# Attention followed by two expert layers on one core: one block of experts beside the attention instead of two, and the third block by seven products

## The chip, the core and the metric

The kernel runs on one core of a Trainium2 chip. The time is the device time of one execution, in microseconds (us); smaller is better. PE is TensorE (matrix products), PEld its weight loads, DVE is VectorE, ACT is ScalarE, POOL is GpSimd, SP is SyncE, which issues the transfers.

## What is computed

An attention with a window of 32 and 32 global tokens per batch, then two layers of the form gate, value, output ("experts") on all 2176 tokens of 512 features, with 1536 hidden features each. Cut to what matters:

```python
x = attention(q_l, k_l, v_l, q_g, k_g, v_g)      # 2176 x 512
xn = x / sqrt(mean(x * x) + 1e-6) * rms_g
g = xn @ w1_gate                                   # 512 x 1536
x = (g * sigmoid(g) * (xn @ w1_val)) @ w1_out      # 1536 x 512
out = (sigmoid(x @ w2_gate) * (x @ w2_val)) @ w2_out
```

All inputs are float64 words in memory, which the kernel turns into float32 and then into pairs of float16 (a high and a low part), so that each product takes three float16 matmuls.

## The kernel before, in words

**Tiling.** The tokens are 17 tiles of 128 (tile 16 holds the global rows). Each expert layer's 1536 hidden features are cut into six blocks of 256; there are 12 blocks, 0 to 11, of which 0 to 5 are the first layer. A block has three weight matrices: gate, value and output.

**Two ways of multiplying a block.** Blocks below `GS` (line 90, 3 before) go in the plain way: the tokens in six chunks of three tiles (the last of two), and for each chunk 48 matmuls for gate and value (`gv_mm`, line 311) and 24 for the output (`out1`, line 496). The output of a chunk comes one chunk late: `flush`, line 1161, is called after the first half (j = 0) of the next chunk. Blocks from `GS` on go through `quad_gv` (line 385): the tokens in three parts of 6, 6 and 5 tiles, each cut in two halves, and gate and value each from seven products of half size in place of eight, that is 84 matmuls of 384 columns (320 for the third part) at line 364, and 48 of the same width for the output. The seven products need sums and differences of the tokens, made once per layer (`x_combos`, line 603, and `combos`, line 579: for each part and each of two halves of the features one group of seven jobs, 42 jobs in all; lines 613, 587, 593 and 596 on POOL, DVE and ACT), and of the weights (`sums`, `sums2` in `w_block`, lines 249 to 255).

**After a half chunk** (`gv_post`, line 322) ACT applies the gate, DVE multiplies, ACT makes the high part and POOL the low part `hlo` (line 343). The output matmuls of `out1` need `hlo` as their second operand already. While attention steps are left, the gate is a Tanh with two products on DVE (lines 337 to 340); after that it is a Silu with one (lines 333, 334).

**Order.** Every engine gets its instructions in an order that the program writes out, and runs them in that order. The attention is a list of 318 steps (about 19 per tile). The first 93 (`n0`, line 1132) run before any expert work. Then the chunks of the list `work` (the list `first`, line 1087, then the chunks of block 2) are emitted one by one, and the function `tick` (line 1106), called 12 times per chunk (four times in each half, four times in `out1`), deals out the rest: at every `pace[2]`-th tick one job of `x_combos`, at every `pace[1]`-th tick one step of the weights' preparation (`w_step`, line 290, from the list that `w_block` fills: ten steps for a plain block, sixteen for one with seven products), and so many attention steps that each chunk's tokens are ready when it comes (`due`, line 1091, from the order of `first`). Counting this through by hand gives, for the order before, 61, 23, 22, 23, 23, 23, 22, 20 and 8 attention steps in the chunks 0 to 8, and none after. `x_combos` enters its jobs when the attention is out of steps, at the start of chunk 9.

**Weights.** DVE shifts and joins the words of the weights (lines 151, 154, 157), ACT makes the high part (line 187), DVE the low part (line 190). `w_need` runs what is missing at once when a block is about to start; `j_need`, line 542, does the same for the token sums before the first block with seven products.

Of the kernel before, what the change touches and what calls it, by code (L numbers as in the profile page):

```python
# [19 lines left out]
def tile_attention_moe_moe(  # L20
# [59 lines left out]
    chunks_b = [(i, o * 128, n * 128) for i, o, n in ((0, 0, 3), (0, 3, 3), (1, 0, 3), (1, 3, 3), (2, 0, 3), (2, 3, 2))]  # L80
# [6 lines left out]
    w_src = [(w1_gate, w1_val, w1_out), (w2_gate, w2_val, w2_out)]  # L87
    wide = w1_gate.dtype == mybir.dt.int64

    GS = 3  # L90

    GP = 6
    raw_t = []
# [80 lines left out]
    def w_half(n, j):  # L174
        w_ahead(2 * n + (j + 3 if wide else 2))
        if wide:
            if len(w_words.get(n, [])) <= j:
                w_scale(n)
            w_bits(n, j, 0)
            w_bits(n, j, 1)  # L180
            w_scale(n + j)
            w_ahead(2 * n + j + 4)
            if j == 1:
                w_words.pop(n)
# [12 lines left out]
    def w_block(g):  # L197
        w_done[g] = [False, False]

        def mark(i):  # L200
            w_done[g][i] = True
# [3 lines left out]
        def small(f):  # L205

            def f2():
                f()
                w_step()
            return f2  # L210

        def late():
            while w_late:
                w_lo(*w_late.pop())

        def conv(w):
            n = 3 * g + w
            if g < GS:
                return [lambda: (late(), w_half(n, 0)), lambda: w_half(n, 1)]
            return [lambda: (late(), w_conv1(n)), lambda: w_conv2(n)]  # L220
# [9 lines left out]

        if g < GS:
            def alloc():
                w_t[g] = [hp.tile([128, 2, 2, 2, DM], F16, tag="wgv", name="wgv"), None]
# [45 lines left out]
        def alloc_o():  # L279
            w_t[g][1] = (hp if g < GS else pb[1]).tile([128, 2, 2, DM], F16, tag="wo", name="wo", bufs=2 if g < GS else 3)  # L280

        jobs += conv(2) + [small(alloc_o), plain(2, lambda: [w_t[g][1][:, :, a] for a in range(2)])]
        if g < GS:
            jobs.insert(wgv_done + 1, small(lambda: mark(0)))
# [799 lines left out]
            pos[0] += 1  # L1084


    first = [(0, 0, 3), (0, 3, 3), (1, 0, 3), (1, 3, 3), (0, 6, 3), (1, 6, 3), (0, 9, 3), (1, 9, 3), (0, 12, 3), (0, 15, 2), (1, 12, 3), (1, 15, 2)]

    MARGIN = 2400
    due = []  # L1090
# [1 line left out]
    work = []  # L1092
# [4 lines left out]
        xi, o = x_place(T)  # L1097
        work.append((g, (xi, o * 128, n * 128), T + n - 1))
    due = due[1:]
    work += [(g, ch, None) for g in range(2, GS) for ch in chunks_b]  # L1100
    clock = [0, 0.0]


    pace = [0, 2, 3]

    def tick(n):
        pace[0] += 1
# [19 lines left out]
    with tc.manual_schedule():  # L1127
        load_k(0)
        load_q(0)
        load_k(1)  # L1130
        setup()
        n0 = done[2] + 4
        W0 = 16
        acts = {
            "kg": lambda: gsrc.update(k=load_g(k_g)),
            "gB": lambda: nc.sync.dma_start(out=gB, in_=rms_g.partition_broadcast(128)),
            "q1": lambda: load_q(1),
            "qg": lambda: gsrc.update(q=load_g(q_g)),
            "v0": lambda: load_v(0),
            "v1": lambda: load_v(1),  # L1140
            "v2": lambda: load_v(2),
            "vg0": lambda: load_vg(0),
            "vw0": lambda: start_vw(0),
            "vw1": lambda: start_vw(1),
            "w0": w_load,
            "w1": w_load,
            "w2": w_load,
        }
        plan = [[0, 'qg'], [3, 'v0'], [8, 'w0'], [0, 'kg'], [0, 'q1'], [4, 'vg0'], [8, 'vw0'], [9, 'w2'], [10, 'gB'], [8, 'w1'], [0, 'v1'], [10, 'v2'], [15, 'vw1']]
        w_block(0)  # L1150
        plan += [(W0 + (n0 - W0) * i // 11, w_step) for i in range(11)]
        plan += [(i, lambda n=n: warm(n)) for i, n in enumerate([13, 2, 2, 2, 2, 10])]
        for i, a in sorted(plan, key=lambda x: x[0]):
            run_to(min(i, n0))
            (acts[a] if isinstance(a, str) else a)()
        run_to(n0)
        clock[1] = float(n0)

        w_block(1)

        def flush():

            while pend:
                g, key = pend.pop(0)
                if g == group[g][-1]:
                    outs(g, key)
                if 0 < g < GS and key in (2, chunks_b[-1], last.get(g)):
                    w_block(g + 2)
                    pace[1] = [2, 4, 3, 3, 4, 4, 4, 2, 4, 2, 2, 2][g]
                if g == NBLK - 1:  # L1170
                    if isinstance(key, int):
                        y_combos(key)
                    elif key[1] > 0:
                        y_combos(key[0])

        last = {g: [w[1] for w in work if w[0] == g][-1] for g in range(2)}
        for wi, (g, ch, ci) in enumerate(work):
            if ci is not None:
                run_to(done[ci])
                clock[1] = max(clock[1], float(pos[0]))  # L1180
            if pos[0] == len(steps) and not pb:
                st_at.close()
                pb[1] = st_p1.enter_context(tc.tile_pool(name="pb1", bufs=1, side="right", reuse_waits="tile"))
                pb[0] = st_p0.enter_context(tc.tile_pool(name="pb0", bufs=1, side="right", reuse_waits="tile"))
                for q in range(3):
                    x_combos(q)
            w_need(g, 0)
            for j in range(2):
                gv_mm(g, ch, j, 0)
                tick(ch[2])  # L1190
                gv_mm(g, ch, j, 1)
                gv_post(g, ch, j)
                tick(ch[2])
                if j == 0 and wi < len(work) - 1:
                    flush()
            pend.append((g, ch))
            if g == 0 and ch == last[0]:
                w_block(2)
        for q in range(3):
            j_need(q, 1)  # L1200
        flush()
        st_p0.close()
        st_pa.close()
        st_ps.close()
        pb["ps"] = st_ps.enter_context(tc.tile_pool(name="pp", bufs=4, space=PSUM, reuse_waits="tile"))
        pb[2] = st_p2.enter_context(tc.tile_pool(name="pb2", bufs=1, reuse_waits="tile"))
        pace[2] = 3
        for gr in GROUPS[GS:]:
            a, b = gr[0], gr[-1]
            for g, q in [(a, q) for q in range(3)] if a == b else [(a, 0), (a, 1), (b, 0), (a, 2), (b, 1), (b, 2)]:  # L1210
                w_need(g, 0)
                j_need(q, 0 if g == GP else 1)
                (plain_gv if g == GP else quad_gv)(g, q, flush)
                if q == 2 and g + 2 < 2 * NBLK:
                    w_block(g + 2)
                    pace[1] = [2, 4, 3, 3, 4, 4, 4, 2, 4, 2, 2, 2][g]
                pend.append((g, q))
        run_deferred()
        flush()
        st_p1.close()  # L1220
        st_p2.close()
        st_ps.close()
# [31 lines left out]
```

## Time and profile before

| what | us |
|---|---|
| median of 3 runs | 941.57 (940.61 to 942.18) |
| the profiled execution | 940.32 |
| its span, first to last instruction | 938.5 |
| PE busy | 883.9 (94%) |
| DVE busy | 661.3 (70%) |
| ACT busy | 368.8 (39%) |
| POOL busy | 337.8 (36%) |

The profile is of one execution. Its span leaves out 1.8 us of the execution's time; the execution lies 1.25 us below the median. Matmuls are pipelined, so a busy PE says that it has work, and the length of a run of matmuls says how fast it does it. A wait is put down to the instruction whose semaphore came last.

### The profile page before, as it was taken

The page shows a single profiled execution, that of the slowest core. Times are in us where ns is not written, and L with a number is a line of the kernel's source. Part 1 is how long each engine was busy: PE and PEld are TensorE (multiplying, and loading weights), DVE is VectorE, ACT ScalarE, POOL GpSimd, SP SyncE. Part 2 cuts the span into 40 slices and gives each one's busy share as a digit, 9 for nine tenths or more (in the row PEclk, how much of TensorE's full clock was granted, in tenths as well). Part 3 has the DMA queues.
Part 4 walks back from the last instruction along what each step waited for, and adds up shares of the span by engine and source line. Part 5 has one row for each costly group of instructions (what it writes and reads, how often), then busy time and mean ns, then how long its engine had stood idle before and what let it go on. Part 6 is the DMA issues. An engine that isn't in the chain of part 4 may idle for free.

```text
span 938.5 us, 19204 instructions
## 1 busy us (share of the span) xinstructions
PE 883.9 (94%) x8119; PEld 549.6 (59%) x8119; DVE 661.3 (70%) x935; ACT 368.8 (39%) x685; POOL 337.8 (36%) x372
## 2 busy tenths in 40 slices
PE   7667899999997997999999799999999999999997
PEld 4455566666675665666666466656556655556553
DVE  2987886646567766899966977737598557997352
ACT  3665566445443333333333344433344213333120
POOL 5548665556254556212221263232111203012120
PEclk9889999999999998999999899999999999999999
DMA  9774453200012111121201121101122011200102
GB/s 192 181 147 96 100 132 69 61 3 2 4 47 90 45 45 45 67 69 45 76 17 45 45 90 46 45 1 46 45 90 90 1 45 46 90 23 1 68 23 101
DMA packets 88999, 58.13 MB, mean 62 GB/s; under 512 B 58449, under 2 KB 83537, under 8 KB 88913
## 3 DMA queue, kind: packets, MB, share of 16 engines
q1 hardware_dynamic: 88912, 56.90, 22.0%
q8 instruction: 64, 1.05, 0.5%
q14 instruction: 23, 0.18, 0.1%
HBM read 52.17 MB, written 4.46 MB: 60 GB/s over the span
## 4 chain that ended last, share of the span: by engine, by line
PE 73%; DVE 16%; issue 3%; POOL 3%; ACT 2%; DMA 2%; SPq 0%; DVEq 0%; ACTq 0%; POOLq 0%
PE p L364 27%; PE p L518 13%; PE b L311 11%; PE p L496 6%; PE b L496 5%; PE p L459 5%; DVE wf L154 3%; PE b L737 2%; DVE wf L157 2%; DVE wf L151 2%; PE b L861 1%; DVE G L418 1%; DVE ya L478 1%; DVE V L418 1%; PE b L806 1%
## 5 line engine op out<-in xcount | busy, mean ns | idle before, releaser
L364 PEld LDWEIGHTS <-wc 128*128 128x128 f16 x2016 | 198.8, 99 | 129.8 <-issue 11.4
L364 PE MATMUL p<-tt,wc 128*128 128x384 f16 (+1 forms) x1152 | 203.3, 320 | 7.0 <-DVE G L418 5.6
L364 PE MATMUL p<-xhi,wc 128*128 128x384 f16 (+1 forms) x576 | 157.9, 320 | 5.2 <-DVE ya L478 5.2
L399 POOL TENSOR_TENSOR h<-V,h 128x1536 f16<-128x1536 f32 (+1 forms) x24 | 71.3, 2971 | 242.4 <-ACT h L398 225.2
L311 PE MATMUL b<-xhi,wgv 128*128 128x384 f16 (+1 forms) x576 | 143.5, 319 | 0.0
L518 PE MATMUL p<-wo,h 128*128 128x512 f16 x612 | 133.5, 379 | 0.0
L496 PEld LDWEIGHTS <-wo 128*128 128x128 f16 x864 | 84.3, 98 | 52.8 <-issue 7.1
L311 PEld LDWEIGHTS <-wgv 128*128 128x128 f16 x864 | 83.0, 98 | 46.6 <-issue 2.4
L518 PEld LDWEIGHTS <-h 128*128 128x128 f16 x612 | 59.8, 98 | 71.3 <-POOL h L399 0.4
L311 PE MATMUL b<-xlo,wgv 128*128 128x384 f16 (+1 forms) x288 | 91.8, 319 | 1.3 <-DVE xlo L911 1.3
L364 PE MATMUL p<-xlo,wc 128*128 128x384 f16 (+1 forms) x288 | 92.2, 320 | 0.0
L478 DVE SCALAR_TENSOR_TENSOR ya<-p,ya 128x768 f32<-128x768 f32 (+3 forms) x42 | 42.3, 1016 | 61.2 <-PE p L518 48.3
L694 POOL COPY vw<-vt 32x520 f32<-32x520 f32 (+1 forms) x92 | 81.0, 881 | 11.2 <-DMA vt<-in_v_l_dram 6.9
L496 PE MATMUL b<-hhi,wo 128*128 128x384 f16 (+1 forms) x288 | 72.7, 320 | 3.4 <-ACT hhi L342 3.4
L425 ACT ACTIVATE sa<-p 128x384 f32<-128x384 f32 (+1 forms) x48 | 22.6, 470 | 135.6 <-PE p L364 115.8
L343 POOL TENSOR_TENSOR hlo<-t,hhi 128x384 f16<-128x384 f32 (+1 forms) x36 | 38.3, 1064 | 92.5 <-ACT hhi L342 92.3
L398 ACT ACTIVATE h<-V 128x1536 f16<-128x1536 f32 (+1 forms) x24 | 33.9, 1413 | 92.8 <-DVE V L397 92.8
L496 PE MATMUL p<-h,wo 128*128 128x384 f16 (+1 forms) x432 | 67.3, 317 | 0.0
L418 DVE TENSOR_TENSOR V<-p,V 128x768 f32<-128x768 f32 (+3 forms) x72 | 56.6, 786 | 12.2 <-PE p L364 9.3
L418 DVE TENSOR_TENSOR G<-p,G 128x768 f32<-128x768 f32 (+3 forms) x72 | 56.5, 785 | 8.7 <-PE p L364 6.4
L157 DVE SCALAR_TENSOR_TENSOR wf<-raw,wf 128x512 int32<-128x512 int32 x72 | 55.8, 806 | 0.6
L154 DVE SCALAR_TENSOR_TENSOR wf<-raw,wf 128x512 int32<-128x512 int32 x72 | 54.1, 783 | 1.6
(137 smaller groups left out, 1311.8 us busy)
## 6 DMA issues: line engine op xcount, KB each, us to landing
raw<-in_moe_w_gate_dram SPq DMA_DIRECT2D x24, 512.0 KB, 4.0
raw<-in_moe_w_val_dram SPq DMA_DIRECT2D x24, 512.0 KB, 4.1
raw<-in_moe_w_out_dram SPq DMA_DIRECT2D x24, 512.0 KB, 4.0
k<-in_k_l_dram SPq DMA_DIRECT2D x16, 256.0 KB, 4.5
q<-in_q_l_dram SPq DMA_DIRECT2D x16, 256.0 KB, 4.2
vt<-in_v_l_dram SPq DMA_DIRECT2D x32, 128.0 KB, 4.6
out_dram<-ya SPq DMA_DIRECT2D x16, 256.0 KB, 2.3
vg<-in_v_g_dram SPq DMA_DIRECT2D x16, 64.0 KB, 4.0
```

The lines of the kernel that those rows point to most:

```text
L154: nc.vector.scalar_tensor_tensor(out=u[:, j], in0=w_words[n][j][:, :, 1], scalar=-0x80000000, in1=u[:, j], op0=ALU.bitwise_and, op1=ALU.bi ...
L157: nc.vector.scalar_tensor_tensor(out=u[:, j], in0=w_words[n][j][:, :, 0], scalar=29, in1=u[:, j], op0=ALU.logical_shift_right, op1=ALU.bit ...
L311: nc.tensor.matmul(p[:, 0:n], wgv[:, j, gv, a, k * 128:(k + 1) * 128], x[xi][:, k, o:o + n], start=(i == 0), stop=(i == 11),)
L343: EH[3].tensor_tensor(out=lo, in0=t, in1=hi, op=ALU.subtract)
L364: nc.tensor.matmul(p, wc[:, w, a, wi, kt * 128:(kt + 1) * 128], r, start=(i == 0), stop=(i == 5))
L399: EH[j // 2].tensor_tensor(out=lo[:, j:e], in0=vj, in1=hi[:, j:e], op=ALU.subtract)
L418: nc.vector.tensor_tensor(out=o, in0=p, in1=i, op=ALU.add)
L459: nc.tensor.matmul(gv[:, w], wc[:, w, a, c, (k % 2) * 128:(k % 2 + 1) * 128], x[q][:, k, h * n:(h + 1) * n], start=(i == 0), stop=(i == 11))
L478: nc.vector.scalar_tensor_tensor(out=ya, in0=p, scalar=1.0 / WS, in1=ya, op0=ALU.mult, op1=ALU.add)
L496: nc.tensor.matmul(p[:, i, 0:n], wo[:, j, a, d * 128:(d + 1) * 128], hh[:, j, ho:ho + n], start=(c == 0), stop=(c == 6 * len(gr) - 1),)
L518: nc.tensor.matmul(p[:, i], hh[:, j, (i0 + i) * 128:(i0 + i + 1) * 128], wo[:, j, a, :], start=(c == 0 and g == gr[0]), stop=(c == 5 and g ...
L694: eng.tensor_copy(out=dst, in_=src)
```

## The change

`GS` becomes 2: blocks 0 and 1 stay plain, block 2 goes through `quad_gv` and its weights are prepared as those of blocks 3 and up. The order of `first` puts four chunks of block 0 in front, then one of block 1, the last two of block 0, and the other five of block 1. The six plain chunks of block 2 leave the list. `tick` makes a weight step at every third tick (second before) until block 0 is done and every second from then on, and an `x_combos` job at every tick (every third before) until the first block with seven products. Ahead of the first chunk nine weight steps are dealt out over the attention's steps in place of eleven (the eleventh found nothing to do before; the tenth now comes after). `w_block(3)` is entered at block 1's last output, as before.

```diff
--- before.py
+++ after.py
@@ -87,7 +87,7 @@
     w_src = [(w1_gate, w1_val, w1_out), (w2_gate, w2_val, w2_out)]
     wide = w1_gate.dtype == mybir.dt.int64
 
-    GS = 3
+    GS = 2
 
     GP = 6
     raw_t = []
@@ -1084,7 +1084,8 @@
             pos[0] += 1
 
 
-    first = [(0, 0, 3), (0, 3, 3), (1, 0, 3), (1, 3, 3), (0, 6, 3), (1, 6, 3), (0, 9, 3), (1, 9, 3), (0, 12, 3), (0, 15, 2), (1, 12, 3), (1, 15, 2)]
+    first = [(0, 0, 3), (0, 3, 3), (0, 6, 3), (0, 9, 3), (1, 0, 3), (0, 12, 3), (0, 15, 2),
+             (1, 3, 3), (1, 6, 3), (1, 9, 3), (1, 12, 3), (1, 15, 2)]
 
     MARGIN = 2400
     due = []
@@ -1097,11 +1098,10 @@
         xi, o = x_place(T)
         work.append((g, (xi, o * 128, n * 128), T + n - 1))
     due = due[1:]
-    work += [(g, ch, None) for g in range(2, GS) for ch in chunks_b]
     clock = [0, 0.0]
 
 
-    pace = [0, 2, 3]
+    pace = [0, 3, 1]
 
     def tick(n):
         pace[0] += 1
@@ -1148,7 +1148,7 @@
         }
         plan = [[0, 'qg'], [3, 'v0'], [8, 'w0'], [0, 'kg'], [0, 'q1'], [4, 'vg0'], [8, 'vw0'], [9, 'w2'], [10, 'gB'], [8, 'w1'], [0, 'v1'], [10, 'v2'], [15, 'vw1']]
         w_block(0)
-        plan += [(W0 + (n0 - W0) * i // 11, w_step) for i in range(11)]
+        plan += [(W0 + (n0 - W0) * i // 9, w_step) for i in range(9)]
         plan += [(i, lambda n=n: warm(n)) for i, n in enumerate([13, 2, 2, 2, 2, 10])]
         for i, a in sorted(plan, key=lambda x: x[0]):
             run_to(min(i, n0))
@@ -1164,7 +1164,7 @@
                 g, key = pend.pop(0)
                 if g == group[g][-1]:
                     outs(g, key)
-                if 0 < g < GS and key in (2, chunks_b[-1], last.get(g)):
+                if g == 1 and key == last[g]:
                     w_block(g + 2)
                     pace[1] = [2, 4, 3, 3, 4, 4, 4, 2, 4, 2, 2, 2][g]
                 if g == NBLK - 1:
@@ -1196,6 +1196,7 @@
             pend.append((g, ch))
             if g == 0 and ch == last[0]:
                 w_block(2)
+                pace[1] = 2
         for q in range(3):
             j_need(q, 1)
         flush()
```

Counted through in the same way, the order after has 66, 58, 51, 22, 20 and 8 attention steps in the chunks 0 to 5; `x_combos` enters its 42 jobs at the start of chunk 6.

## Rows read from the trace of the kernel before

**Rows 1.** Page, part 2: the span in 40 slices, busy tenths by engine

```profile
PE   7667899999997997999999799999999999999997
DVE  2987886646567766899966977737598557997352
POOL 5548665556254556212221263232111203012120
```

**Rows 2.** Stretches: us, busy PE PEld DVE ACT POOL, PE clock, DMA share, GB/s

```profile
71.73:110.17 38.44, 31.23 (x697) 21.96 (x691) 30.16 (x60) 23.48 (x66) 29.20 (x49) 0.96 0.55 110
110.17:132.52 22.35, 20.40 (x330) 13.07 (x328) 20.06 (x32) 12.35 (x31) 12.61 (x15) 0.92 0.36 105
132.52:151.80 19.28, 18.67 (x316) 12.30 (x308) 14.49 (x22) 12.04 (x36) 14.23 (x20) 1.00 0.43 93
151.80:259.42 107.62, 107.62 (x1651) 71.75 (x1646) 60.46 (x134) 50.35 (x133) 50.64 (x81) 1.00 0.11 23
...
278.98:304.43 25.45, 20.20 (x146) 14.07 (x145) 19.80 (x31) 10.23 (x20) 11.02 (x9) 1.00 0.32 102
304.43:356.47 52.04, 52.04 (x338) 32.87 (x337) 36.89 (x57) 19.72 (x34) 28.94 (x23) 1.00 0.13 41
...
363.15:372.80 9.65, 4.42 (x14) 2.02 (x14) 7.07 (x13) 2.49 (x4) 4.56 (x3) 0.65 0.01 2
```

**Rows 3.** Chain that ended last, in order of time: start us, us, what

```profile
300.69 7.80 PE b L311 x48
308.49 3.90 PE b L496 x24
...
418.62 7.80 PE p L496 x48
426.42 13.65 PE p L364 x84
```

**Rows 4.** Waits, 270 to 300 us: who for whom, us in total, times, longest

```profile
PE b L496 <- ACT hhi L342: 3.4, 2, 2.5
PE b L496 <- POOL hlo L343: 1.8, 2, 1.1
```

**Rows 5.** Waits, 356 to 376 us

```profile
PE p L364 <- DVE ya L478: 5.2, 1, 5.2
```

**Rows 6.** Timeline of PE from 363 us: start, us, instruction, idle before

```profile
368.97 0.84 PE L364 MATMUL p<-xhi,wc 128*128 128x384 f16 x2
...
372.81 0.49 PE L364 MATMUL p<-xhi,wc 128*128 128x384 f16 x2
```

**Rows 7.** Timeline of POOL, 301.8 to 336 us

```profile
301.93 2.41 POOL L613 TENSOR_TENSOR xb<-xhi,xlo 128x768 f32<-128x768 f16 x1
305.89 1.47 POOL L343 TENSOR_TENSOR hlo<-t,hhi 128x384 f16<-128x384 f32 x1 [1.54 <-ACT hhi L342]
...
317.59 0.93 POOL L343 TENSOR_TENSOR hlo<-t,hhi 128x384 f16<-128x384 f32 x1 [2.01 <-ACT hhi L342]
318.48 1.64 POOL L596 TENSOR_TENSOR tt<-xb,tt 128x768 f16<-128x768 f32 x1
...
322.72 1.64 POOL L613 TENSOR_TENSOR xb<-xhi,xlo 128x768 f32<-128x768 f16 x1
...
334.49 1.00 POOL L587 TENSOR_TENSOR xb<-xb 128x384 f32<-128x384 f32 x1
```

**Rows 8.** Timeline of DVE, 301.8 to 312 us

```profile
301.89 0.96 DVE L613 TENSOR_TENSOR xb<-xhi,xlo 128x768 f32<-128x768 f16 x1 [0.74 <-POOL tt L596]
...
305.89 2.01 DVE L154 SCALAR_TENSOR_TENSOR wf<-raw,wf 128x512 int32<-128x512 int32 x2
307.83 0.94 DVE L587 TENSOR_TENSOR xb<-xb 128x768 f32<-128x768 f32 x1
```

**Rows 9.** Weight lines, 257 to 370 us: duration ns min/median/max, first and last start

```profile
L154 DVE SCALAR_TENSOR_TENSOR wf<-raw,wf x14: 683/692/1405, 269.6 to 369.6; 128x512 int32<-128x512 int32 x14
L190 DVE SCALAR_TENSOR_TENSOR wc<-wf,wc x2: 1212/1214/1217, 320.8 to 344.9; 128x1024 f16<-128x1024 f32 x2
```

## The prediction

> **What bounds the kernel now.** The page's slices come first [rows 1]. From the sixth slice (117 us) on PE is at nine tenths or more nearly everywhere, so there the time is the sum of the matmuls, and any matmul saved counts. Before that PE is at six to eight tenths while DVE and POOL are high: there the attention's order sets the pace. The kernel is then cut at the starts of its chunks [rows 2]. Chunk 0 (71.73 to 110.17) takes 38.44 us, of which PE is busy 31.23. Chunks 3 to 8 (151.80 to 259.42) are PE without a gap at full clock. From 278.98 to 304.43 PE lacks 5.25 us, from 304.43 to 356.47 nothing, and after 363.15 it stands again and then runs at half clock.
>
> Prices of PE at full clock: 48 matmuls of 384 columns 7.80, 24 take 3.90, the 84 of a part with seven products 13.65, their 48 for the output 7.80 [rows 3]. A plain chunk of three tiles is thus 11.7, one of two tiles two thirds of it, 7.8. The six chunks 3 to 8 are 70.2 of the 107.62 us [rows 2]; the other 37.4 carry 119 attention steps, 0.314 us of PE each.
>
> **The change part by part.** *Products.* Block 2 in the plain way is five chunks of 11.7 and one of 7.8: 66.3 us. With seven products its parts are 21.45, 21.45 and five sixths of that, 60.8. Minus 5.5, on the path, as PE is full there. DVE has room for the extra additions: the stretch where blocks 3 to 5 run already that way keeps PE mostly at nine tenths with DVE at six to nine [rows 1].
>
> *The wait before block 2.* Near 282 and 296 us PE waits 3.4 and 1.8 us for the high and low parts [rows 4]: `w_block(2)` is entered after chunk 9, and its ten steps must go through DVE, together with token sums, during two short chunks. After the change there are five chunks between, so this wait goes: minus 5.2. What takes its place is the backlog below.
>
> *The step into seven products.* PE waits 5.2 us for DVE's late accumulations [rows 5], because eight of the 42 token jobs were left and `j_need` put them all in front of them. Then the clock is half until 372.8: two matmuls take 0.84 us, and 0.49 from there on [rows 6]. The 4.4 us at the lower level hold some 14 matmuls that lose 0.16 each, 2.2 us. After the change the jobs are long done. I leave 1.0 us for the last accumulation. Minus 6.4, bounds minus 7.4 and minus 3.
>
> *The attention with less beside it.* By PE alone (7.8 for chunk 0, 11.7 each for the others, 0.314 per step) chunks 0, 1 and 2 of before would be 27.0, 18.9 and 18.6; they take 38.44, 22.35 and 19.28 [rows 2], so 15.5 are lost. In chunks 0 and 1 DVE is busy 30.16 and 20.06, POOL 29.20 and 12.61: three engines with nearly the same load, that wait for each other. After the change that density lasts three chunks in place of one (66, 58, 51 steps): by PE 28.5, 29.9 and 27.7. Chunk 0 at its 0.63 us per step is 41.6; two weight steps fewer on DVE (about 1.9 each) make it 37.8, a loss of 9.3. The other two have PE and DVE about level, as chunk 1 had, which took 1.18 times PE's sum: 35.3 and 32.7, a loss of 5.4 and 5.0; chunks 3 to 5 add 0.7. That is 20.4 for 15.5: plus 4.8. Bounds: minus 6 (three chunks at 1.10) and plus 21 (all three at chunk 0's ratio of 1.42).
>
> *Start.* One weight step moves out of the first 72 us, where DVE is the fullest engine [rows 1]: minus 1.5, bounds minus 3 and 0.
>
> *The backlog, the largest unknown.* From chunk 6 the 42 jobs come at every tick, and `w_block(2)` at every second from chunk 7. One group of seven jobs at its undisturbed durations is on POOL 1.64, 1.00 and twice 1.64 [rows 7], on DVE 0.95, 0.94 and about 0.54 [rows 8], and it is one chain: 8.3 us for the seven ticks in which PE needs 6.8. A group of the third part is 6.9. Besides, POOL must make `hlo` of every half chunk (0.92, of the short chunk 0.66), and DVE the weights: twelve of 0.68, two of 1.21, two of 0.95 (by width), one more of 1.21 [rows 9], and some 4 us of small ones, 20.3 for 16 steps.
>
> Do the two engines run beside each other? POOL's line 613 starts at 301.93, just after DVE's at 301.89, and takes 2.41 where 1.64 is usual; DVE's took its usual 0.96 [rows 7, 8]. At 305.89 `hlo` and the first of two L154 start together: `hlo` takes 1.47 for 0.93, the pair 2.01 for 1.37 [rows 7 to 9]. Each waited for the other to end. The Trainium skill says so too (SBUF — State Buffer, "Who interferes with whom"): a DVE instruction with two SBUF inputs contends with a GpSimd instruction that reads SBUF, and the second "fully blocks". The trace agrees, and it speaks against this change, which packs just such instructions.
>
> `hlo` of chunk 8's second half stands in POOL's queue behind 36 jobs, and PE needs it 4.6 us into chunk 9: by PE alone 9.1 + 10.4 + 11.7 + 4.6 = 35.8 us after chunk 6 began. Ahead of it lie four groups and one of the third part plus one job, 41.5, and seven low parts, 5.9; POOL begins 1.5 us in. So 48.9 if all weight steps hide, a wait of 13; with 11 weight steps (14.0) strictly in between 62.9, a wait of 27; and if POOL and DVE did not hinder each other, POOL's own 29.9 + 5.9 + 1.5 = 37.3, a wait of 1.5. I take 17: nearer to the chain, as it also waits for ACT, when weight steps cost nothing. After tick 42 no jobs come, and the rest of block 1 is PE alone.
>
> *Block 2 as the first with seven products* has a few small waits of its own: plus 0.9, bounds 0 and 3.
>
> **Sum.** 5.5, 5.2, 6.4 and 1.5 off, 4.8, 17 and 0.9 on: plus 4.1. The span of 938.5 becomes 942.6, the profiled execution's 940.32 becomes 944.4. It lay 1.25 below the median of 941.57, so the median becomes 945.7, slower by 0.4%.
>
> **The rivals.** *The backlog is absorbed.* If POOL and DVE slip past each other better than the rows at 302 and 306 us suggest, the wait is about 4 and the rest of the sum stands: 932.7. For it speaks that from 304.43 to 356.47, with a third of the jobs per tick and weights too, PE has no gap; against it that DVE and POOL were busy 36.89 and 28.94 of those 52.04 us already [rows 2]. Faster.
>
> *A draw.* With a backlog near the chain's own 13 the sum is plus 0.1: 941.7.
>
> *The attention jams.* If the ratio of chunk 0, 1.42, holds for all three dense chunks, since PE, DVE and POOL there hold each other, the loss grows to some 37: 962. This decides once the steps come faster than one in 0.6 us, the pace of chunk 0 of before. For it speaks that chunk; against it chunk 1, with a chunk's worth of matmuls to fill the gaps.
>
> That the products save nothing is no rival: their number follows from the code, and PE is full where they run.
>
> **How the numbers follow.** A measurement of this kernel can tell about 0.2%, 1.9 us, from no change. Forecast (backlog of some 15 to 25, 943.5 to 956): 0.46. Backlog absorbed: 0.33. Draw: 0.13. Jam: 0.08. So faster 0.33, same 0.13, slower 0.54. The range reaches from 930, where the backlog is at its lower bound of 1.5, to 957, with it at 27 and a little over: it leaves out most of the jam and the tail of the faster cases. The forecast's own range is 943.5 to 956.
>
> **What would show it.** Right: in the last five plain chunks PE waits on `hlo` (POOL, line 343), 10 us or more in all, with POOL and DVE full there and line 343 taking more than 0.93; the waits near 282 us and the one of 5.2 at the first seven products are gone, and no half clock follows; the dense chunks take 105 us together. Wrong: PE without gaps in the last plain chunks (then the backlog is small and the kernel faster), or dense chunks of 40 us each (the jam), or a wait for block 2's weights in place of `hlo`.

## The result: 1.45% slower

The kernel with the change takes 954.97 us (953.22 to 955.81, four runs), the kernel before, run beside it, 941.09 (940.07 to 942.18): a ratio of 1.0145 [1.0126, 1.0164]. The sign is the forecast's and the time lies inside its range, near the upper end; the size is not: +13.9 where +4.1 was expected. The profiled execution took 953.22; its span is 951.43, 13.0 us more than the 938.47 of before. The account below is of these two profiled executions.

The profile after, cut at the starts of its chunks, answers to [rows 2]. Columns: stretch, its us, busy time (and instructions) of PE, its weight loads, DVE, ACT and POOL, PE clock, DMA share, GB/s. The first three lines are the dense chunks 0 to 2, the fourth is 3 to 5, then come chunks 6 to 9, and the last two chunks before block 2 in one line:

```profile
70.37:106.26 35.89, 31.23 (x758) 22.55 (x758) 27.83 (x57) 22.20 (x68) 28.51 (x46) 1.00 0.58 116
106.26:142.35 36.09, 30.89 (x657) 21.69 (x657) 31.59 (x54) 24.04 (x68) 27.38 (x43) 1.00 0.45 104
142.35:182.03 39.68, 33.32 (x736) 23.39 (x730) 26.47 (x52) 22.14 (x60) 25.83 (x37) 0.87 0.38 78
182.03:230.29 48.26, 48.26 (x613) 31.45 (x611) 27.25 (x59) 25.20 (x61) 20.31 (x29) 1.00 0.01 3
230.29:239.43 9.14, 9.14 (x74) 7.04 (x73) 3.18 (x5) 4.39 (x9) 5.83 (x6) 1.00 0.00 0
239.43:254.72 15.29, 12.12 (x74) 7.64 (x72) 8.89 (x10) 4.41 (x10) 12.01 (x7) 0.89 0.01 2
254.72:278.67 23.95, 14.47 (x75) 7.75 (x73) 21.75 (x21) 8.55 (x14) 18.15 (x14) 0.79 0.21 69
278.67:299.06 20.39, 14.53 (x73) 7.78 (x72) 17.31 (x23) 7.98 (x13) 15.59 (x11) 0.83 0.17 55
299.06:322.60 23.54, 23.54 (x170) 16.37 (x168) 10.19 (x17) 5.61 (x12) 5.62 (x7) 1.00 0.05 18
```

By PE alone chunk 7 (with the outputs of the short chunk 6) would last 10.4, chunks 8 and 9 11.7 each; they last 15.29, 23.95 and 20.39, and in chunk 8 DVE is busy 21.75 of 23.95 and POOL 18.15. That is where most of the time came from. The account of the whole, before to after:

| what | us | forecast |
|---|---|---|
| start of the first chunk, 71.73 to 70.37 | −1.4 | −1.5 |
| attention: loss against PE's own sum, 15.64 in chunks 0 to 8 of before, 22.97 in 0 to 5 of after | +7.3 | +4.8 |
| seven products for eight in block 2 | −5.5 | −5.5 |
| wait before block 2 (103.7 for PE's 97.5) | −6.2 | −5.2 |
| backlog: block 1's chunks without attention, 230.29 to 322.67, 92.4 for PE's 66.3 | +26.1 | +17 |
| step into seven products (5.23 of waiting and 2.2 of lower clock before, nothing after) | −7.4 | −6.4 |
| the rest | +0.1 | +0.9 |

Two rows have less behind them than the others. The one on the products is a count of PE's own times; what is measured is that row and the rest together. And the start is one profile against one: fourteen kernels below run the same program up to the first chunk as the kernel after, and it starts there between 70.1 and 73.6, so a gain of 1.4 is not shown.

Block 1's stretch as one. PE stands 18.5 of its 92.4 us and is busy 73.87 for its 66.3, so 7.6 of the 26.1 are matmuls at a lower granted clock (0.89 over the stretch):

```profile
230.29:322.67 92.38, 73.87 (x458) 46.65 (x457) 61.36 (x74) 30.94 (x56) 57.19 (x41) 0.89 0.11 35
```

Waits after, 232 to 324 us (engine, line, whom it waits for: us in total, times, longest), answering to [rows 4]:

```profile
ACT hhi L342 <- DVE t L334: 21.0, 12, 4.1
...
PE b L496 <- ACT hhi L342: 16.2, 3, 8.9
...
PE b L496 <- POOL hlo L343: 2.3, 3, 1.3
```

PE does stand before block 1's outputs, as forecast, but 16.2 us of it is for the high part from ACT and only 2.3 for `hlo` from POOL. ACT in its turn waits 21.0 us for DVE's product. The last link was DVE as much as POOL. The longest of these waits, in the timelines of DVE, POOL, ACT and PE (start, us, instruction, idle before and its releaser):

```profile
260.45 1.75 DVE L255 TENSOR_TENSOR sm<-wf,sm 128x256 f32<-128x256 f32 x1
262.12 2.65 DVE L190 SCALAR_TENSOR_TENSOR wc<-wf,wc 128x1024 f16<-128x1024 f32 x1
264.69 2.38 DVE L613 TENSOR_TENSOR xb<-xhi,xlo 128x768 f32<-128x768 f16 x1
267.00 0.55 DVE L334 SCALAR_TENSOR_TENSOR t<-b,t 128x384 f32<-128x384 f32 x1
```

```profile
260.10 3.59 POOL L596 TENSOR_TENSOR tt<-xb,tt 128x768 f16<-128x768 f32 x2
263.77 2.49 POOL L613 TENSOR_TENSOR xb<-xhi,xlo 128x768 f32<-128x768 f16 x1
```

```profile
267.58 0.52 ACT L342 ACTIVATE hhi<-t 128x384 f16<-128x384 f32 x1 [4.13 <-DVE t L334]
```

```profile
268.15 0.48 PE L496 MATMUL b<-hhi,wo 128*128 128x384 f16 x1 [8.88 <-ACT hhi L342]
...
287.73 0.48 PE L496 MATMUL b<-hhi,wo 128*128 128x384 f16 x1 [4.52 <-ACT hhi L342]
289.55 0.48 PE L496 MATMUL b<-hlo,wo 128*128 128x384 f16 x1 [1.34 <-POOL hlo L343]
...
322.67 0.33 PE L364 MATMUL p<-xhi,wc 128*128 128x384 f16 x1
```

Line 334 of DVE takes 0.55, but it stands in the queue behind a weight step of 2.65 (1.21 undisturbed [rows 9]) and a token sum of 2.38 (0.96 [rows 8]); POOL's sum beside it takes 2.49 for 1.64 [rows 7]. Neither engine looks idle in these rows: the hindrance is inside the durations. PE stands 8.88 us. The last release, at 289.55, comes 59.3 us after chunk 6 began; the last line is the step into seven products, now without a wait before it and at full clock, where [rows 5, 6] had 5.2 and a half clock.

### The profile page after: what moved, and what is told of

The parts are those of the page before. It is cut to its first block, busy times and chain, and to the rows that moved or that the text cites. A ratio compares the mean times of both kernels' runs of the same rounds, so it can differ in the third digit from the quotient of the medians.

```text
span 951.4 us, 19130 instructions
## 1 busy us (share of the span) xinstructions
PE 884.3 (93%) x8083; PEld 548.0 (58%) x8083; DVE 695.0 (73%) x935; ACT 370.4 (39%) x675; POOL 339.7 (36%) x367
## 4 chain that ended last, share of the span: by engine, by line
PE 71%; DVE 14%; POOL 6%; issue 4%; ACT 3%; DMA 1%; SPq 1%; ACTq 0%; DVEq 0%; POOLq 0%
PE p L364 33%; PE p L518 14%; PE p L496 8%; PE b L311 4%; PE p L459 4%; PE b L496 3%; POOL vw L694 2%; PE b L737 2%; DVE wf L154 1%; POOL tt L596 1%; DVE wf L157 1%; DVE wf L151 1%; DVE wc L190 1%; POOL hlo L343 1%; PE b L861 1%
## 5 line engine op out<-in xcount | busy, mean ns | idle before, releaser
L364 PEld LDWEIGHTS <-wc 128*128 128x128 f16 x2268 | 222.8, 98 | 136.4 <-issue 6.7
L364 PE MATMUL p<-tt,wc 128*128 128x384 f16 (+1 forms) x1296 | 227.7, 319 | 5.9 <-DVE G L418 4.5
L364 PE MATMUL p<-xhi,wc 128*128 128x384 f16 (+1 forms) x648 | 176.5, 318 | 0.0
L496 PEld LDWEIGHTS <-wo 128*128 128x128 f16 x864 | 86.3, 101 | 71.3 <-issue 26.1
L364 PE MATMUL p<-xlo,wc 128*128 128x384 f16 (+1 forms) x324 | 103.1, 318 | 0.0
L311 PE MATMUL b<-xhi,wgv 128*128 128x384 f16 (+1 forms) x384 | 95.4, 318 | 0.5 <-ACT xhi L904 0.4
L496 PE MATMUL p<-h,wo 128*128 128x384 f16 (+1 forms) x576 | 90.0, 317 | 0.0
L418 DVE TENSOR_TENSOR V<-p,V 128x768 f32<-128x768 f32 (+3 forms) x81 | 63.7, 786 | 16.4 <-PE p L364 13.9
L311 PEld LDWEIGHTS <-wgv 128*128 128x128 f16 x576 | 54.8, 98 | 31.0 <-issue 1.1
L496 PE MATMUL b<-hhi,wo 128*128 128x384 f16 (+1 forms) x192 | 54.3, 350 | 16.2 <-ACT hhi L342 16.2
L311 PE MATMUL b<-xlo,wgv 128*128 128x384 f16 (+1 forms) x192 | 60.9, 317 | 0.4 <-DVE xlo L911 0.4
L154 DVE SCALAR_TENSOR_TENSOR wf<-raw,wf 128x512 int32<-128x512 int32 x72 | 59.3, 858 | 1.5
L249 POOL TENSOR_TENSOR sm<-wf 128x256 f32<-128x256 f32 x18 | 13.7, 763 | 125.1 <-DVE wf L157 125.1
```

The lines of the kernel that those rows point to most:

```text
L154: nc.vector.scalar_tensor_tensor(out=u[:, j], in0=w_words[n][j][:, :, 1], scalar=-0x80000000, in1=u[:, j], op0=ALU.bitwise_and, op1=ALU.bi ...
L311: nc.tensor.matmul(p[:, 0:n], wgv[:, j, gv, a, k * 128:(k + 1) * 128], x[xi][:, k, o:o + n], start=(i == 0), stop=(i == 11),)
L364: nc.tensor.matmul(p, wc[:, w, a, wi, kt * 128:(kt + 1) * 128], r, start=(i == 0), stop=(i == 5))
L418: nc.vector.tensor_tensor(out=o, in0=p, in1=i, op=ALU.add)
L496: nc.tensor.matmul(p[:, i, 0:n], wo[:, j, a, d * 128:(d + 1) * 128], hh[:, j, ho:ho + n], start=(c == 0), stop=(c == 6 * len(gr) - 1),)
```

## The experiments

In the texts on record, theory A is that POOL's work and DVE's work on operands in SBUF add up, since one engine shuts the other out; the other letters are rivals, described where they stand. "Block 1's stretch" is chunk 6 to the first matmul of line 364, 92.4 us in the kernel after; "dense chunks" are chunks 0 to 2, 111.7 us there. The texts on record call the kernels e1 to e15; the headings have the numbers. Each ratio is to the kernel before, run beside it (medians of 941.84, 941.86, 941.0 and 942.18 in the four groups of runs). Stretches and waits are read from one profiled execution of each kernel.

**Thin out the jobs (e1).** The kernel after, with an `x_combos` job at every second tick:

```diff
-    pace = [0, 3, 1]
+    pace = [0, 3, 2]
```

> The changed kernel with one number different: a token job at every second tick in place of every tick. Theory A (the backlog: token jobs and weight steps ask more of POOL and DVE per tick than PE's time): the stretch from the end of the attention to the end of block 1, 92.5 us in the changed kernel where PE's own work is 66.3, falls to about 72; eight jobs are left over and the wait before the first seven products comes back, some 5 to 7 us. Time about 941 us, 936 to 946. Theory B (the weight steps on DVE alone make the stretch long): the stretch stays above 85, time 950 to 957. Theory C (the dense attention is the loss): nothing changes there, 955.

941.21 us, 0.9995 [0.9985, 1.0006]: one number takes back the whole loss. The dense chunks stay (111.2), block 1's stretch falls from 92.4 to 78.5 (less far than the 72 expected), which includes a wait of 2.7 before the first seven products, where eight jobs are left over. So the packing of the backlog costs some 14 us, and the jam of the attention doesn't depend on it.

**The order without the products (e2).** The kernel before with the new order of `first`, its nine early steps and its two paces of weight steps; jobs stay at every third tick and block 2 stays plain:

```diff
-    GS = 2
+    GS = 3
...
-    pace = [0, 3, 1]
+    pace = [0, 3, 3]
```

(against the kernel after, with the chunks of block 2 back in the list, and the line that enters the next block's weights as before)

> The kernel before with the new order of chunks and the new pace of weight steps, but block 2 still multiplied in the plain way and a token job at every third tick. Theory A: the attention's part costs 5 to 6 us more than before (1.4 less at the start, 7 more in the dense chunks), the wait before block 2 (5.2) and the late accumulations with their half clock (7.4) go, no backlog: about 935 us, 931 to 939, faster than both kernels. Theory C (the dense attention is where the time goes): 946 or more.

938.14, 0.9967 [0.9952, 0.9983]. The dense chunks take 111.8, as in the kernel after; the wait near 282 and the one before seven products are gone. The half of the change that puts one block beside the attention is worth 3.7 us without the other half.

**Which work makes the backlog (e3, e4).** Block 2's joins (lines 151, 154, 157) left out, so that its weights stay unjoined words, and, in a second kernel, replaced by shifts of the same size with one input:

```diff
     def w_bits(n, j, k):
+        if n in (6, 7, 8):
+            return
```

```diff
+            if one:                       # one = n in (6, 7, 8)
+                nc.vector.tensor_scalar(out=u[:, j], in0=w_words[n][j][:, :, 1 - k], scalar1=3, scalar2=None,
+                                        op0=ALU.logical_shift_right)
```

> The changed kernel, leaving out lines 151, 154 and 157 for block 2: its weights keep only what ACT makes of the upper words, 15 DVE instructions less, 10.2 us at their undisturbed durations. Theory A (POOL and DVE in one sum): the stretch of block 1 gets shorter by about as much, time 944 to 947. Theory D (POOL's queue alone is the backlog): under 3 us less, 952 to 955. Theory B: the loss of the stretch falls by more than half, 940 to 944.

949.95 (two runs, 948.18 and 951.71; the profile is of the first), 1.0089 [1.0064, 1.0114]; block 1's stretch 88.6, 3.8 shorter: between theories A and D, a miss for both. Four of the twelve joins could give nothing: in the kernel after they stand behind the last release, at 292.9 and 295.0 us, where PE no longer waits. The other eight are 5.4 us at 0.68.

> The changed kernel with the twelve joins of block 2 (lines 154 and 157, two inputs from SBUF) put in as shifts of one input from SBUF with the same stride; the weights' bits of block 2 are not what they should be. If the instruction lasts as long (0.55 to 0.69 us) DVE has the same work, and only what two inputs do to POOL is gone. Theory A with mutual waiting: POOL's instructions beside them fall back to their undisturbed durations and the stretch gets 5 to 8 us shorter, 947 to 950. Theory B (DVE's own load): within 2 us of the changed kernel, 953 to 956.

951.48, 1.0105 [1.0085, 1.0126]; stretch 90.4. This told nothing apart, because the shifts turned out not to be free of POOL: the same form took 0.41 at best and 1.86 at worst.

**Move the token jobs (e5, e6).** All token jobs on DVE, and all on POOL (ACT's part unchanged):

```diff
+    EX = [nc.vector] * 8          # second kernel: nc.gpsimd
...
-            EG[i].tensor_tensor(out=o, in0=i0, in1=i1, op=ALU.subtract)
+            eg[i].tensor_tensor(out=o, in0=i0, in1=i1, op=ALU.subtract)
```

(and so in lines 596 and 613, for the token jobs alone)

> The changed kernel with all POOL instructions of the token jobs (lines 613, 587 and 596) given to DVE. A group of seven jobs is then about 5.9 us on DVE alone, by the 0.95 us that DVE takes for 768 columns, in place of 8.3 on both. Theory A (POOL and DVE use one thing in turn, so what counts is the sum of both): the sum before the low part of chunk 8 falls from 63 to about 51 and the loss of the stretch from 26 to about 15: 943 to 947. Theory B (DVE's own load is the bound, as PE waits for what follows DVE's product): DVE gets some 20 us more to do in the stretch, 960 or more.

> The changed kernel with all DVE instructions of the token jobs given to POOL. A group is then about 10.2 us on POOL alone (1.64 for 768 columns, 1.0 for 384); DVE has 14 us less in the stretch. Theory A: the sum grows by some 10 us, 962 to 968. Theory B (DVE's own load): the loss falls by about half, 940 to 946.

947.05 on DVE, 1.0053 [1.0033, 1.0073]; 967.9 on POOL, 1.0275 [1.0254, 1.0295]. Block 1's stretch of the one and of the other:

```profile
233.17:318.30 85.13, 72.04 (x456) 46.02 (x455) 68.67 (x98) 30.70 (x56) 18.46 (x17) 0.92 0.12 38
```

```profile
233.47:337.90 104.43, 74.84 (x458) 46.99 (x456) 50.14 (x56) 31.14 (x56) 80.27 (x59) 0.84 0.10 31
```

With 24 more instructions on DVE, the engine that PE was found waiting for, the stretch is 7 us shorter (a loss of 18.8, where about 15 was expected); with 18 fewer it is 12 longer. DVE as a bound by its own load falls. DVE's busy time rises by only 7.3 (from 61.36) while POOL's falls by 38.7 (from 57.19): much of what the kernel after books as DVE's work was standing.

**The exclusion by itself (e12).** No part of the computation; eight subtractions on POOL (128x768, both operands in SBUF) and sixteen operations on DVE, each alone and then both together:

```diff
+    nc.gpsimd.tensor_tensor(out=a, in0=f, in1=h, op=ALU.subtract)                # x8
+    nc.vector.tensor_tensor(out=b, in0=h, in1=h1, op=ALU.add)                    # x16: two inputs in SBUF
+    nc.vector.scalar_tensor_tensor(out=b, in0=psum, scalar=0.5, in1=f, ...)      # x16: one of two in PSUM
+    nc.vector.tensor_scalar(out=b, in0=f, scalar1=1.5, scalar2=None, op0=ALU.mult)   # x16: one input
```

> No part of the computation: seven stretches one after the other, with 8 POOL instructions of the form of line 596 (two inputs from SBUF, 768 columns) and 16 of DVE of the same width, alone and beside each other. POOL alone 8 times 1.64, 13.1 us; DVE with two inputs from SBUF alone 16 times 0.95, 15.2. If they exclude each other (theory A) both together take about 28 us; if they only share, some 15 to 20. With one of DVE's inputs from PSUM: no hindrance, about 16 us together. With one input from SBUF (a scalar product): if e4's 0.41 to 1.86 us is the same exclusion, the sum of both again, 13 plus about 7; if not, 13.

Its timelines of POOL and DVE (start, us for the whole row of operations):

```profile
2.15 13.63 POOL L60 TENSOR_TENSOR a<-f,h 128x768 f16<-128x768 f32 x8 [1.71 <-DVE h L48]
35.84 17.79 POOL L60 TENSOR_TENSOR a<-f2x,h2x 128x768 f16<-128x768 f32 x8 [20.05 <-ACT f2x L89]
83.32 13.66 POOL L60 TENSOR_TENSOR a<-f4x,h4x 128x768 f16<-128x768 f32 x8 [29.69 <-ACT f4x L89]
114.68 15.37 POOL L60 TENSOR_TENSOR a<-f6x,h6x 128x768 f16<-128x768 f32 x8 [17.70 <-ACT f6x L89]
```

```profile
17.42 15.85 DVE L66 TENSOR_TENSOR b<-h1x,h 128x768 f32<-128x768 f16 x16 [14.33 <-ACT h1x L87]
34.92 26.48 DVE L66 TENSOR_TENSOR b<-h2x,h 128x768 f32<-128x768 f16 x16 [1.64 <-ACT h2x L87]
64.93 15.83 DVE L72 SCALAR_TENSOR_TENSOR b<-pbank,f3x 128x768 f32<-128x768 f32 x16 [3.53 <-ACT f3x L93]
83.27 15.84 DVE L72 SCALAR_TENSOR_TENSOR b<-pbank,f4x 128x768 f32<-128x768 f32 x16 [2.52 <-ACT f4x L89]
102.64 9.48 DVE L78 TENSOR_SCALAR b<-f5x 128x768 f32<-128x768 f32 x16 [3.53 <-ACT f5x L93]
114.64 19.99 DVE L78 TENSOR_SCALAR b<-f6x 128x768 f32<-128x768 f32 x16 [2.52 <-ACT f6x L89]
```

Two inputs in SBUF: 15.85 and 13.63 alone, 26.48 together, nine tenths of the sum. POOL also takes longer, 17.79, so neither engine simply goes first. With one operand in PSUM: 15.84 and 13.66, nothing lost. With one input: 9.48 alone, 19.99 beside POOL.

**Spread the weight steps thinner (e7, e8).** The order alone, with a weight step at every fourth tick, and the kernel after with jobs at every second tick and weight steps at every fourth:

```diff
-    pace = [0, 3, 3]              # second kernel: [0, 3, 1]
+    pace = [0, 4, 3]              # second kernel: [0, 4, 2]
...
-                pace[1] = 2
+                pace[1] = 4
```

> As e2 (block 2 plain, new order), with the weight steps at every fourth tick both beside the attention and after it. Theory A: the 2 us wait of PE near 256 us in e2 goes, and the dense chunks get a step or two of weights less: 934 to 937, about 2 to 4 us under e2. If the dense chunks are bound by the attention's own steps and not by the weights, 938 as e2.

947.11, 1.0061 [1.0038, 1.0083]: a miss, 9 us slower than with every third tick. Chunk 2 alone takes 44.35, for 39.68 in the kernel after. A weight step of DVE fell on a worse place there (0.42, 0.69 and 0.69 are the shortest rows of lines 151, 154 and 157):

```profile
142.58 1.39 DVE L190 SCALAR_TENSOR_TENSOR wgv<-wf,wgv 128x1024 f16<-128x1024 f32 x1
143.90 2.51 DVE L151 TENSOR_SCALAR wf<-wf 128x512 int32<-128x512 int32 x1
146.44 0.99 DVE L154 SCALAR_TENSOR_TENSOR wf<-raw,wf 128x512 int32<-128x512 int32 x1
147.46 0.99 DVE L157 SCALAR_TENSOR_TENSOR wf<-raw,wf 128x512 int32<-128x512 int32 x1
```

The attention's maximum of line 821 begins at 148.37, behind all four; line 828 of ACT needs it, and PE stands 5.15 for line 828. A chunk of block 1 (tiles 12 to 14) lost another 5 (16.86 for 11.7), but the order alone had lost 4 at another chunk of block 1 (15.67). The four runs lie at 945 and 949, and the profile is of the shortest.

> The changed kernel (block 2 by seven products) with token jobs at every second tick and weight steps at every fourth, beside the attention and after it. Theory A: of the 9.5 us that block 1's stretch loses in e1 and the 3 before the first products about half is left: 934 to 938, faster than before by what the products save. If the sum of POOL's and DVE's work in the stretch is the bound however it is dealt out: 940 to 942, as e1.

946.56 (939.84 to 947.9), 1.0031 [1.0009, 1.0053]: a miss too. Its ten runs lie in two groups, three near 940.5 and seven near 947; what divides them was not found. The profile is of the shorter group (939.84): there chunk 2 takes the same 44.3 and block 1's stretch is down to 75.4. What the other seven lose stands in no profile.

**Both, with the token jobs on DVE (e9, e10).** Weight steps at every third tick beside the attention; from block 2's weights on every fourth, with jobs at every second, and the order alone with its jobs on DVE:

```diff
-    pace = [0, 3, 1]
+    pace = [0, 3, 2]
...
-                pace[1] = 2
+                pace[1] = 4
```

(with the diff of the token jobs on DVE; for the order alone that diff and nothing else)

> The changed kernel (block 2 by seven products) with three things different: token jobs at every second tick, weight steps after the attention at every fourth, and the token jobs all on DVE. Weight steps beside the attention at every third tick, as in the changed kernel. Theory A (the sum of POOL's and DVE's work in the stretch of block 1): that sum falls by 14 us against e1, the stretch loses 3 us or less of PE's time, the eight jobs left over cost 3 to 6 before the first products: 933 to 938, faster than before. If seven products cannot pay here: 940 or more.

> As e2 (block 2 plain, new order), with the token jobs all on DVE. Theory A: the wait of 2 us near 256 us and the 2 us of slow matmuls after it get shorter or go: 934 to 938. If that wait is made by the weight steps alone: 938 as e2.

938.16, 0.9967 [0.9953, 0.9981], and 937.46, 0.9957 [0.9945, 0.997]. The first has block 1's stretch at 74.1, where PE stands 5.66 before the first seven products, again for eight jobs left over. The second lies 0.7 under the order alone, less than these measurements can tell apart.

**What slows the attention (e11).** The kernel after, with block 1's joins left out, so that its weights stay unjoined words:

```diff
+        if n in (3, 4, 5):
+            return
```

> The changed kernel, leaving out lines 151, 154 and 157 for block 1, whose steps stand beside the dense attention: its weights keep only what ACT makes of the upper words. 18 DVE instructions less, some 10.8 us undisturbed. Theory A for the dense chunks (weight steps on DVE and the copies of the attention on POOL hold each other up): chunks 0 to 2, 111.7 us in the changed kernel, get 7 to 12 us shorter, time 943 to 948. Theory E (the attention's own steps set the pace): 2 us or less, 952 to 956.

937.0, 0.9954 [0.9937, 0.9971]. The dense chunks, 111.66 us in the kernel after (its first three lines above), as one stretch of this one:

```profile
72.35:166.74 94.39, 90.93 (x2150) 65.34 (x2145) 66.97 (x143) 66.88 (x191) 77.72 (x124) 1.00 0.53 114
```

Six weight steps lost three operations each, 6 x (0.42 + 0.69 + 0.69) = 10.8 us by their shortest rows, and PE got 17.3 back. With the same attention steps beside the same chunks PE is now busy 90.93 of 94.39; by PE's own sum they would take 86.1, so 8.3 of the 25.6 lost are left. Both theories on record had bet on less. How such a step costs more than itself is seen in the kernel after near 156 us; DVE, POOL, PE:

```profile
154.22 1.61 DVE L190 SCALAR_TENSOR_TENSOR wgv<-wf,wgv 128x1024 f16<-128x1024 f32 x1
155.76 0.84 DVE L151 TENSOR_SCALAR wf<-wf 128x512 int32<-128x512 int32 x1
156.63 1.86 DVE L154 SCALAR_TENSOR_TENSOR wf<-raw,wf 128x512 int32<-128x512 int32 x1
158.52 1.92 DVE L157 SCALAR_TENSOR_TENSOR wf<-raw,wf 128x512 int32<-128x512 int32 x1
160.36 0.28 DVE L751 COPY kT<-b 128x128 f32<-128x128 f32 x1
```

```profile
153.71 3.36 POOL L694 COPY vw<-vt 64x1040 f32<-64x1040 f32 x3
158.85 2.07 POOL L694 COPY vw<-vt 64x1040 f32<-64x1040 f32 x2
```

```profile
161.96 0.40 PE L799 MATMUL b<-mask,ident 32*32 32x256 bf16 x4 [6.07 <-ACT kT L756]
```

One step's four operations last 6.2 us in place of 3.0, beside POOL's copies, and line 751, which PE's chain needs and which takes 0.28, stands behind them.

**Hold block 1's weights back (e13 to e15).** No weight step by pace until chunk 3, then one at every second tick; on the kernel after, on the order alone with jobs on DVE, and on the spread products with jobs on DVE:

```diff
-    pace = [0, 3, 1]              # second kernel: [0, 3, 3], third: [0, 3, 2]
+    pace = [0, 1000, 1]           # second kernel: [0, 1000, 3], third: [0, 1000, 2]
...
+            if wi == 3:
+                pace[1] = 2
             w_need(g, 0)
```

> The changed kernel with the weight steps of block 1 held back until chunk 3 (none beside chunks 0 to 2; from chunk 3 on at every second tick, what is missing at chunk 4 at once). Nothing is left out. If e11's 17 us came from where the joins stood (beside dense attention steps and POOL's copies), moving them gives most of it: chunks 0 to 2 about 97 us in place of 111.7, up to 4 us lost in chunks 3 to 5 where PE is full and DVE has room, time 940 to 947. If what counts is the work itself, wherever it stands, the time moves out of chunks 0 to 2 and comes back in 3 to 6: 951 or more.

> e10 (block 2 plain, new order, token jobs on DVE) with the weight steps held back as in e13. With the place of the steps as the cause: 923 to 929, clearly faster than before. With the work itself as the cause: 935 to 939, as e10.

> e9 (block 2 by seven products, token jobs on DVE at every second tick, later weight steps at every fourth tick from block 2 on) with the weight steps of block 1 held back as in e13. With the place of the steps as the cause: 922 to 930, equal to e14 within 3 us: what the products save, 5.5, is about what the eight token jobs left over cost at the first of them. With the work itself as the cause: 936 to 940, as e9.

948.49, 1.0071 [1.0053, 1.009] on the kernel after, 6.5 us less than it; 929.92, 0.9877 [0.9852, 0.9902] on the order alone; 931.76, 0.9893 [0.9875, 0.991] with seven products. All three lie 0.9 to 1.8 us above the range for the place as the cause and 2.5 to 5.1 under the other. The stretches of dense chunks, of chunks 3 to 5 and of what follows, in the first and the second of them:

```profile
72.46:172.81 100.35, 93.70 (x2152) 66.87 (x2145) 66.93 (x141) 61.59 (x184) 76.28 (x124) 0.97 0.36 76
172.81:227.34 54.53, 50.73 (x611) 32.27 (x610) 42.01 (x79) 30.91 (x70) 22.10 (x29) 0.97 0.20 61
227.34:319.90 92.56, 71.65 (x460) 45.83 (x458) 61.34 (x74) 30.92 (x56) 57.21 (x41) 0.91 0.11 35
```

```profile
72.34:171.09 98.75, 92.21 (x2153) 65.83 (x2146) 66.74 (x141) 61.46 (x184) 76.03 (x124) 0.98 0.37 78
171.09:226.03 54.94, 50.55 (x611) 31.99 (x610) 42.01 (x79) 30.76 (x70) 22.05 (x29) 0.97 0.20 60
226.03:361.70 135.67, 133.31 (x889) 86.77 (x887) 99.17 (x155) 48.71 (x89) 31.50 (x29) 1.00 0.15 47
```

The dense chunks give back 11 to 13 us, chunks 3 to 5 take 6 to 7 of that, as block 1's steps now press there (2.7 of it is PE's wait for block 1's weights); the backlog, untouched in the first kernel, stays (92.4 to the first matmul of line 364).

The edit does one thing more than its heading says. The pace also deals out the last, tenth step of block 0, which makes the low part of its output weights; held back too, it runs only when the first output needs it. In the kernel after it ran at 80.7 us, in the first kernel here at 116.8, for 3.50 us where 1.21 is usual, and PE stands 5.16 for it (5.1 in the other two):

```profile
116.76 3.50 DVE L190 SCALAR_TENSOR_TENSOR wo<-wf,wo 128x1024 f16<-128x1024 f32 x1
```

So these three kernels carry a wait that has nothing to do with block 1's weights. A kernel without it was not run.

The second kernel beats both kernels of the case, by 1.2% over the one before. The seven products add nothing to it, the third is 1.8 us slower: 73.8 of block 1's stretch for PE's 66.3 (5.34 of it before the first product) loses 7.5, while the plain version loses 3.1 in its 135.67 for 132.6; that difference is 4.4 of the products' 5.5. Besides, behind the wait of 5.34 the granted clock is 0.55 until 306.00, 5.42 us, which costs some 2.4 more (an estimate: 5.42 x 0.45); in the second kernel it is 1.00 at that place.

## Why the prediction was partly right

**Right, within 1 us each:** the wait before block 2, the step into seven products, and the products together with block 2's own small waits. These were terms with one place and one price, read from rows of the same work. The start came out as forecast too, but one profile each cannot show 1.5 us there.

**The backlog, mis-sized: 17 forecast, 26.1 measured.** The mechanism is the one named: jobs and weight steps packed on POOL and DVE, which shut each other out (thinning the jobs took 14 us back; moving them off POOL helped and onto POOL hurt; the two run alone and together in nine tenths of the sum of their times). What failed is the step "I take 17: nearer to the chain, as it also waits for ACT, when weight steps cost nothing". PE was to need the last `hlo` at 35.8 us after chunk 6 began; the release came at 59.3, against 48.9 for the chain and 62.9 for the strict sum. So 23.5 of the term lay before the release, where the strict sum had 27, and 2.6 behind it, in the rest of chunk 9 at the lower clock, which the sum had not counted (the granted clock is 0.83 in that chunk). The rows at 302 and 306 us [rows 7, 8], where each engine waited for the other to end, were the evidence for the strict sum, and they were read and then discounted. The strict sum had its own slips. The parts named for the weights add up to 17.7 us and not to 20.3; and what POOL does for the weights was put at nothing, lines 249 and 250, four instructions of 0.72 before the release. From undisturbed rows the weights before the release are 12.8 on DVE and 2.9 on POOL, 15.7 for the 14.0 of the sum, so the strict sum is 64.6 and still an upper bound.

The Trainium skill (SBUF — State Buffer, "SBUF: two separate sides") calls the ports that the two engines share an exclusive lock, not a division of bandwidth. The trace of the two alone agrees but for a tenth: 26.48 together, where a full lock would give 29.48 and no hindrance 15.85. Why the tenth is missing was not followed.

What the forecast said of the place was half right. It had PE wait on `hlo` for 10 us or more; PE waited 2.3 for it and 16.2 for the high part. The low part was thought late because POOL's queue is long. In fact DVE's queue was held up by POOL, so that the product which both parts are made from came late, and with it the high part first.

**The attention, mis-sized: 4.8 forecast, 7.3 measured.** The dense chunks took 35.89, 36.09 and 39.68 where 37.8, 35.3 and 32.7 were expected. Against PE's own sum they lost 25.6, forecast 19.7; chunks 3 to 5 took 2.5 less than that sum where 0.7 more was forecast, which hides part of the miss. The step that failed is the ratio of 1.18 for the later two chunks; the third came out at 39.68 / 27.7 = 1.43. Its reason failed in the main too: "three engines with nearly the same load, that wait for each other". Without block 1's joins the same steps beside the same chunks lose 8.3, so density explains no more than that (and in chunk 1 of before POOL was busy only 12.61 of 22.35). The other 17.3 go with the joins, and most of it goes too when they are only moved. At the two places that were followed, four weight operations stand ahead of a short link of the chain on DVE while POOL copies; that it is the same in general is argued, not shown. Which steps fall badly hangs on the count of ticks: every fourth tick was worse than every third.

**The rivals.** The backlog absorbed and the draw fell with 92.4 for 66.3. The jam (three dense chunks at 1.42) came true for one chunk of three.

**Open.** Leaving out block 2's joins gave 3.8 us in block 1's stretch, where a strict sum wants at least the 5.4 of the eight joins before the last release; so that sum is an upper bound, and what filled the room was not found. Nor was the kernel run that holds back block 1's weights and not the last step of block 0.

## What to carry to other kernels

Where POOL and DVE work on operands in SBUF in the same stretch, add their undisturbed times and compare the sum with PE's time there, as an upper bound: two engines at half load each can be nearly one engine at full load (26.48 for 29.48 here). With one of DVE's operands in PSUM nothing was lost. Ask of every filler that is dealt out by a counter what short link of the critical chain stands behind it in the queue; a filler can cost more than its own time there (17.3 us for 10.8). A saving on PE counts only after the work that makes it possible has found room: seven products for eight saved their 5.5 us, and even in the best version with them their sums cost 4.4 of it, and the wait that they left some 2.4 more in clock.

## What was not expected of the hardware

An operation of DVE with a single input can be shut out as well: multiplication by a scalar, float32 in SBUF, 128x768, 0.59 us each alone and 1.25 beside POOL (9.48 and 19.99 for sixteen). The rule that the forecast cites is on those with two inputs. The page of the Trainium skill named above lists, besides those with two inputs, DVE's operations in a mode with two ports. That the scalar product runs in such a mode is not shown by any row; that it takes 0.59 where the operation with two inputs takes 0.99 would fit.

POOL suffers too, though less: 17.79 for 13.63 beside two inputs, 15.37 beside one. In the one operation tried with an operand in PSUM (scalar times PSUM, plus SBUF) the hindrance is gone altogether (15.84 and 13.66), although it too reads one operand from SBUF. So the number of inputs from SBUF does not decide it alone.
